# Heads of two pairs change places in the rows of y and x; past terms as products on quarters of the array

## The chip, the cores and the metric

The kernel runs on one core of a Trainium2 chip. The metric is the device time of one execution in microseconds; the median of three runs before the change is 200.99 us (200.46 to 201.04). Lower is better.

Words used below: TensorE multiplies matrices and writes to PSUM, an accumulator memory of banks of 2 KB per partition; VectorE (DVE), ScalarE (ACT) and GpSimd (POOL) do the elementwise work; SyncE (SP) issues most of the transfers (DMA), POOL those of k. A product has a stationary operand, loaded into the array beforehand (a weight load, PEld), and a moving one that streams through it. Where an operand has 64 rows (contraction) or 64 columns (output partitions), only half or a quarter of the 128 x 128 array is used, and products on different parts can run side by side; the profile writes such forms as rows*columns, 128*64, 64*128 or 64*64.

## The reference

```python
# q, k, v: (B=4, H=8, S=768, D=64)
gamma = 1.0 - 2.0 ** (-5.0 - np.arange(H))
for t in range(S):
    state = gamma * state + outer(k[t], v[t])         # per batch and head, 64 x 64
    y[t] = (1 / sqrt(D)) * (q[t] @ state)
x = y.transpose(0, 2, 1, 3).reshape(B * S, H * D)      # 3072 tokens x 512
h = x @ w_in                                           # 512 -> 2048
g = h * np.tanh(softplus(h))                           # mish
out = g @ w_out                                        # 2048 -> 512
```

## The kernel before

**Chunks and heads.** The 768 tokens of a batch are cut into 6 chunks (NCH) of 128 tokens (C), 24 chunks in all, numbered g. Within a chunk, y has a *present* term, from the masked scores of the chunk's own tokens, and a *past* term, q times the state that the chunk before handed on; a chunk that opens a batch has no past term. The 8 heads go in 4 pairs (HP); pair i holds heads 2i and 2i+1, of 64 columns each, so that a pair fills 128 partitions: row block 64*hh is head 2i+hh. The scaling by gamma is put into q and v when they are cast to fp16 (qs, vs).

**y and x.** y is built transposed in PSUM: partition is the row within a pair, then pair, chunk and token. Copied to fp16 it is xt, whose pair index is also the block of 128 rows of w_in (bp) that it meets in the first matrix product. So the order of heads within a pair is the order of the rows of w_in within a block.

**Blocks.** The first block takes 4 chunks, with its own layout of tokens (functions with `first` or `two` in their name), the ten others 2 chunks each, beginning at chunks 4, 6, 8 and so on to 22. For a block, g1_seven computes the product with w_in and seven the one with w_out, by seven products of halves in place of eight for most of the work, with sums of operands on VectorE (x_sums, win_sums, sums_a and so on). A table of steps (steps_of, steps_of_first) names places in those two functions ("p2", "p7", "m1", "m2", "m5", "m7") at which work of the next chunks is issued. Engines execute in the order in which this code issues.

**State.** Two layouts exist. A *wide* state is [128, pair, 128] with the two heads of a pair on the diagonal blocks and zeros elsewhere, so that one product on the whole array serves a pair. A *compact* state, stcs[g], is [128, pair, 64]: head 2i+hh at partitions 64*hh on. Through chunk 4 the states are wide (state_first, and outer_wide and decay_wide with the mask gcm). From chunk 5 on outer makes compact sums in PSUM, state_sum and state_decay (VectorE, POOL) make stcs[g], in three rotating buffers, and spread_state copies it by two ScalarE copies (L435) into one of three wide buffers stx that POOL has zeroed at the start (L112).

**y of a block.** y_two issues the present products of two chunks (present, L463: whole contraction of 128 tokens, 64 output partitions, so two halves of the columns side by side), then the outer products of two later chunks (outer_two, L412), then the past products (past, L454: 4 per chunk on the whole array). It is called at step "m7" inside seven, between two groups of products with w_out (L727); ScalarE copies y to xt (L500).

**Weights and loads.** load_w reads w_in in four slices of 512 columns into staging buffers of [128, 4 blocks, 512]; slices 0 and 1 in two transfers of 256 columns, slices 2 and 3 in one (L158). In SP's queue they stand behind q, k and v of the first block and ahead of w_out (L165), the q and v of chunks 4 and 5 (L140), the last quarter of w_out in two halves (L170, cast by ScalarE at L186) and the further loads. The first slice's first half is cast to fp16 by POOL (L176), the rest by VectorE.

Of the kernel before, what the change touches and what calls it, by code (L numbers as in the profile page):

```python
# [16 lines left out]
def kernel(  # L17
# [67 lines left out]
    stx = [cpool.tile([P, HP, P], FP16, name=f"stx{i}") for i in range(3)]  # L85
# [20 lines left out]
    nc.vector.memset(gcm, 0.0)  # L106
    for h in range(H):
        o = 64 * (h % 2)
        nc.vector.memset(gcm[o:o + 64, h // 2, o:o + 64], float(gamma[h] ** C))
        nc.vector.memset(gcv[o:o + 64, h // 2:h // 2 + 1], float(gamma[h] ** C))  # L110
    decay = gcv.unsqueeze(2).broadcast_to((P, HP, D))
    for t in stx:  # L112
        nc.gpsimd.memset(t, 0.0)
# [39 lines left out]
    def load_w(which, s):  # L153
        if which == "in":
            t = wstage.tile([P, NBP, TB], FP32, name="wi", tag="wt", bufs=4)
            n = TB // 2 if s < 2 else TB
            for o in range(0, TB, n):
                nc.sync.dma_start(t[:, :, o:o + n], win_ap[:, :, s * TB + o:s * TB + o + n])  # L158
        else:
            if s < NSL // 2:  # L160
                t = wstage.tile([P, FPS, d_model], FP32, name="wt", tag="wt", bufs=4)
            else:
                t = gp.tile([P, FPS, d_model], FP32, name="wt", tag="g")
            if s < NSL - 1:
                nc.sync.dma_start(t, wout_ap[:, s * FPS:(s + 1) * FPS])  # L165
        wtmps[which, s] = t
# [70 lines left out]
    def cast_two(nm, s, half):  # L237
        src = raw.pop((nm, s, half))
        if nm == "k":
            if s not in k16s:  # L240
                k16s[s] = castp.tile([P, 2, R, HP, D], FP16, name="qk16")
            nc.scalar.copy(k16s[s][:, half].rearrange("p r h d -> p h r d"), src)
        else:
            v16s[s, half] = castp.tile([P, R, HP, D], FP16, name="v16")
            nc.gpsimd.tensor_tensor(
                v16s[s, half].rearrange("p r h d -> p h r d"), src,
                vs_two[:, half * HP:(half + 1) * HP].unsqueeze(3).broadcast_to((P, HP, R, D)),
                op=ALU.mult)
# [56 lines left out]
    def present_first(s, y, pairs):  # L305
        for i in pairs:
            half, j = divmod(i, HP // 2)
            for r in range(R):
                for c in range(2):
                    for hh in range(2):  # L310
                        nc.tensor.matmul(
                            y[64 * hh:64 * hh + 64, c, i], v16s[s, half][toks(c), r, 2 * j + hh],
# [118 lines left out]
    def spread_state(g):  # L431
        states[g] = stx[g % 3]
        for hh in range(2):
            o = slice(64 * hh, 64 * hh + 64)
            nc.scalar.copy(states[g][o, :, o], stcs[g][o])  # L435

    def outer_wide(g):
        _, k16, v16, _ = cast[g]
        u_ps = u_tile()[:, 0]
        for i in range(HP):  # L440
            nc.tensor.matmul(
                u_ps[:, i], k16[:, 2 * i:2 * i + 2], v16[:, 2 * i:2 * i + 2],
                start=True, stop=True)
# [7 lines left out]
    def past(g, y):  # L451
        st, qt = states[g - 1], qkts[g][0]
        for i in range(HP):
            nc.tensor.matmul(  # L454
                y(i), st[:, i], qt[:, i], start=False, stop=True, skip_group_check=True)

    def present(g, y, fresh):
        am = ams[g]
        v16 = cast[g][2]
        for i in range(HP):  # L460
            for hh in range(2):
                o = 64 * hh
                nc.tensor.matmul(  # L463
                    y(i)[o:o + 64], v16[:, 2 * i + hh], am[:, hh, i],
# [242 lines left out]
    def seven(blk, steps, last):  # L707
# [53 lines left out]
        step("m5")  # L761
# [259 lines left out]
    def spread_next(g):  # L1021
        if g in stcs:
            spread_state(g)

# [6 lines left out]
    def steps_of(blk):  # L1031
# [3 lines left out]
        else:  # L1035
# [6 lines left out]
            "p7": [(store_due, 2), (sum_next, a - 2), (spread_next, a - 3), (sums_a, blk, slice(0, FPS))],  # L1042
# [5 lines left out]
            "m5": only((spread_next, a - 2)),  # L1048
# [4 lines left out]
    def steps_of_first(blk):  # L1053
# [8 lines left out]
            "m1": [(spread_next, a - 2), (scores, a - 2), (scores, a - 1), (mask, a - 2)],  # L1062
# [44 lines left out]
```

## Time and profile before

| what | value |
|---|---|
| median of three runs | 200.99 us |
| the profiled execution | 200.17 us |
| its span, first to last instruction | 198.4 us |
| granted TensorE clock | 1.00 |
| PE busy | 190.2 us, 96% of the span |
| DVE, ACT, POOL busy | 144.8, 114.9, 82.5 us |
| moved by DMA | 36.05 MB |
| past products on wide copies (L454 from stx) | 60, 4.9 us busy |
| past products of chunks 4 and 5 (L454 from st) | 8 |
| present products (L463) | 160, 6.4 us busy |
| copies of states (L435) | 30, 402 ns each, 57.7 to 178.7 us |

How to read it. The span is what the profile covers; the time of an execution has some 1.8 us more around it. Busy times of products overlap, since a product's record covers its passage through the array and the next one starts long before that ends; the step from one start to the next is what a product costs in a stream. In the timeline a line gathers a run of like instructions: start, time from the first start to the last end, engine, line, operation, the array form rows*columns, operand shape and count, and in brackets the idle time ahead of it with its releaser. In the chain of waits each piece has its start and its length; "SPq" is SP's queue of instructions, and DMA is a transfer that was waited for. In the table by windows the DMA share is the mean share of time for which the sixteen DMA engines had packets in hand; packets that overlap on an engine count twice, so it can exceed 1.

### The profile page before, as it was taken

To read this page: it belongs to the slowest core of one execution; us is meant where nothing else is said; L and a number is where in the kernel's file an instruction comes from. 1 tells how busy PE (TensorE), PEld (TensorE's weight loads), DVE (VectorE), ACT (ScalarE), POOL (GpSimd) and SP (SyncE) were. 2 spreads that over 40 slices of the span, in tenths; PEclk is the share of its full clock that TensorE was granted. 3 is DMA by queue.
4 is the path that set the end of the run, shared out by engine and by line. 5 is a ranking of instruction groups with operands and counts; after the bars stand their busy time and mean duration, and the time that the engine had idled before them with its cause. 6 is when DMAs were issued, how large, how long until landed. Compare 5 with 4: busy or idle time off the path is not lost.

```text
span 198.4 us, 5725 instructions
## 1 busy us (share of the span) xinstructions
PE 190.2 (96%) x2363; PEld 157.7 (79%) x2363; DVE 144.8 (73%) x294; ACT 114.9 (58%) x220; POOL 82.5 (42%) x110
## 2 busy tenths in 40 slices
PE   6897999999999999999999999999999999999992
PEld 2355546974987988988988988988988988988982
DVE  3786698998898597597498597597498596596362
ACT  2463667243673675675664774774754765765840
POOL 7072005695646708708606707707615614110000
PEclk9999999999999999999999999999999999999999
DMA  5999999999999999997997996997996967201102
GB/s 170 302 311 354 384 388 318 196 298 176 166 259 225 180 188 226 202 145 156 188 162 156 157 168 146 179 176 93 244 195 84 202 90 61 102 3 53 56 26 79
DMA packets 95897, 36.05 MB, mean 182 GB/s; under 512 B 82304, under 2 KB 89984, under 8 KB 95872
## 3 DMA queue, kind: packets, MB, share of 16 engines
q1 hardware_dynamic: 74928, 33.04, 76.3%
q0 software_dynamic: 20800, 2.62, 21.0%
q8 instruction: 18, 0.29, 0.7%
q14 instruction: 7, 0.06, 0.1%
q10 hardware_dynamic: 144, 0.03, 0.1%
HBM read 27.30 MB, written 6.29 MB: 169 GB/s over the span
## 4 chain that ended last, share of the span: by engine, by line
PE 78%; SPq 7%; DMA 6%; DVE 4%; ACT 2%; issue 1%; DVEq 0%
PE o_ps L727 30%; PE h_ps L654 18%; PE h_ps L630 16%; SPq L140 5%; DMA wt<-in_moe_w_out_dram 4%; PE y_ps L463 3%; PE at L397 3%; DMA qfirst<-in_q_dram 2%; PE y_ps L454 2%; PE o_ps L924 2%; PE h_ps L798 1%; SPq L165 1%; PE u_ps L412 1%; DVE gsum L705 1%; SPq L170 1%
## 5 line engine op out<-in xcount | busy, mean ns | idle before, releaser
L654 PE MATMUL h_ps<-xt,win 128*128 128x256 f16 x320 | 41.5, 273 | 0.0
L647 DVE TENSOR_TENSOR hsum<-h_ps,hsnap 128x512 f32<-128x512 f32 x30 | 19.8, 688 | 20.9 <-PE h_ps L630 18.9
L727 PEld LDWEIGHTS <-gsum 128*128 128x128 f16 x320 | 30.8, 98 | 4.0 <-DVE gsum L705 0.4
L654 PEld LDWEIGHTS <-win 128*128 128x128 f16 x320 | 29.3, 98 | 3.6
L727 PE MATMUL o_ps<-tmat,gsum 128*128 128x256 f16 x240 | 27.8, 273 | 0.0
L727 PEld LDWEIGHTS <-g 128*128 128x128 f16 x240 | 23.3, 98 | 2.9
L641 ACT ACTIVATE g<-hsum 128x512 f16<-128x512 f32 x30 | 18.6, 630 | 11.4 <-DVE hsum L647 11.2
L403 DVE TENSOR_TENSOR am<-at,tri 128x1024 f16<-128x1024 f32 x20 | 24.3, 1215 | 0.0
L347 POOL TENSOR_TENSOR v<-vf,qvs 128x512 f16<-128x512 f32 x20 | 23.5, 1177 | 0.4 <-PE o_ps L924 0.4
L661 ACT ACTIVATE g<-h_ps 128x512 f16<-128x512 f32 x40 | 22.9, 603 | 0.8 <-PE h_ps L654 0.6
L637 ACT COPY hsnap<-h_ps 128x512 f32<-128x512 f32 x30 | 16.4, 582 | 11.2 <-PE h_ps L630 11.2
L336 POOL TENSOR_TENSOR qk<-qf,qvs 128x512 f16<-128x512 f32 x20 | 21.6, 1080 | 2.1 <-DMA qf<-in_q_dram 2.1
L355 POOL COPY gate<-gsum 128x1 f16<-128x1 f16 x9 | 1.6, 183 | 48.4 <-DVE gsum L701 48.4
L741 DVE TENSOR_TENSOR osb<-o_ps,snap 128x256 f32<-128x256 f32 x30 | 12.5, 418 | 12.4 <-PE o_ps L727 10.9
L733 ACT COPY snap<-o_ps 128x256 f32<-128x256 f32 x30 | 11.2, 372 | 16.0 <-PE o_ps L727 15.7
L630 PEld LDWEIGHTS <-wsum 128*128 128x128 f16 x320 | 19.5, 98 | 0.5
L727 PE MATMUL o_ps<-wout,g 128*128 128x256 f16 x160 | 19.3, 273 | 0.0
L342 POOL DMA_DIRECT2D qk<-in_k_dram x20 | 18.8, 942 | 0.0
L630 PE MATMUL h_ps<-xsum,wsum 128*128 128x128 f16 x240 | 16.7, 219 | 0.0
L500 ACT CAST xt<-y_ps 128x1024 f16<-128x1024 f32 x10 | 10.1, 1013 | 10.6 <-PE y_ps L454 10.6
L630 PEld LDWEIGHTS <-win 128*128 128x128 f16 x240 | 15.1, 98 | 0.7
L435 ACT COPY stx<-stc 64x256 f16<-64x256 f16 x30 | 12.0, 400 | 2.0 <-POOL stc L429 1.8
(119 smaller groups left out, 306.9 us busy)
## 6 DMA issues: line engine op xcount, KB each, us to landing
vf<-in_v_dram SPq DMA_DIRECT2D x24, 256.0 KB, 5.7
out_dram<-osb SPq DMA_DIRECT2D x22, 256.0 KB, 4.9
qf<-in_q_dram SPq DMA_DIRECT2D x20, 256.0 KB, 5.4
wt<-in_moe_w_out_dram SPq DMA_DIRECT2D x3, 1024.0 KB, 8.9
qk<-in_k_dram POOLq DMA_DIRECT2D x20, 128.0 KB, 5.5
wi<-in_moe_w_in_dram SPq DMA_DIRECT2D x4, 512.0 KB, 7.3
wi<-in_moe_w_in_dram SPq DMA_DIRECT2D x2, 1024.0 KB, 11.3
qfirst<-in_q_dram SPq DMA_DIRECT2D x2, 512.0 KB, 5.1
```

The lines of the kernel that those rows point to most:

```text
L336: nc.gpsimd.tensor_tensor(room16(g)[0], loaded[g][0], qs.unsqueeze(2).broadcast_to((P, H, D)), op=ALU.mult)
L342: nc.gpsimd.dma_start(room16(g)[1], k[b, :, c * C:(c + 1) * C].rearrange("h p d -> p h d"))
L347: nc.gpsimd.tensor_tensor(room16(g)[2], loaded[g][2], vs.unsqueeze(2).broadcast_to((P, H, D)), op=ALU.mult)
L403: nc.vector.tensor_tensor(am, ats.pop(g), tri.unsqueeze(1).unsqueeze(1).broadcast_to((P, 2, HP, C)), op=ALU.mult)
L630: nc.tensor.matmul(h_ps[:, f], w(f, d), x(d), start=first and f == 0 and d == 0, stop=d == n - 1, skip_group_check=True)
L637: nc.scalar.copy(x, h_ps)
L641: nc.scalar.activation(gt[:, 2 * i * FPS:(2 * i + 1) * FPS, j * P:(j + 1) * P], h, AF.Mish, scale=inv_boost3)
L647: nc.vector.tensor_tensor(h, h_ps, x, op=ALU.add)
L654: nc.tensor.matmul(h_ps[:, j], win(s, 2 * half + j, bp), xt(blk, bp), start=bp == 0, stop=bp == NBP - 1)
L661: nc.scalar.activation(gt[:, fb:fb + 2], h_ps, AF.Mish, scale=inv_boost3)
L727: nc.tensor.matmul(o_ps, x(f), w(f), start=first and f == 0, stop=f == n - 1, skip_group_check=True)
L741: nc.vector.tensor_tensor(dst, o_ps, plus, op=ALU.add)
```

## The change

For pairs 2 and 3 the two heads change places in the rows of y, x and so of w_in: head 2i goes to the upper 64 partitions and head 2i+1 to the lower (`side`). Rows of the state, q and k stay where they are, so in pairs 2 and 3 a state's rows and its columns lie in different halves.

- past: from chunk 7 on, a product per head from the compact state (64 rows of contraction, 64 output partitions) in place of one per pair from a wide copy; pairs in the order 0, 2, 1, 3, so that four products running use the four quarters of the array. The buffers stx, their memsets, spread_state and its three places in the tables of steps go.
- present and present_first write each head's output to its new side; the mask gcm has its blocks there, and outer_wide makes its sums head by head, there.
- cast_two puts the heads of v's second half in swapped order, by two POOL instructions.
- load_w: blocks 0 and 1 of w_in in one transfer as before, blocks 2 and 3 in two transfers of 64 partitions that swap the halves; eighteen transfers in place of six.

```diff
-    stx = [cpool.tile([P, HP, P], FP16, name=f"stx{i}") for i in range(3)]
...
+    def side(i, hh):
+        o = 64 * (hh if i < HP // 2 else 1 - hh)
+        return slice(o, o + 64)
...
-        nc.vector.memset(gcm[o:o + 64, h // 2, o:o + 64], float(gamma[h] ** C))
+        e = side(h // 2, h % 2)
+        nc.vector.memset(gcm[o:o + 64, h // 2, e], float(gamma[h] ** C))
...
-    for t in stx:
-        nc.gpsimd.memset(t, 0.0)
...
-            n = TB // 2 if s < 2 else TB
+            n, hb = (TB // 2 if s < 2 else TB), NBP // 2
             for o in range(0, TB, n):
-                nc.sync.dma_start(t[:, :, o:o + n], win_ap[:, :, s * TB + o:s * TB + o + n])
+                src = win_ap[:, :, s * TB + o:s * TB + o + n]
+                nc.sync.dma_start(t[:, :hb, o:o + n], src[:, :hb])
+                for x in range(2):
+                    nc.sync.dma_start(
+                        t[64 * x:64 * x + 64, hb:, o:o + n],
+                        src[64 * (1 - x):64 * (1 - x) + 64, hb:])
...
+            if half == 0:
+                nc.gpsimd.tensor_tensor(dst, src, f, op=ALU.mult)
+            else:
+                for hh in range(2):
+                    nc.gpsimd.tensor_tensor(
+                        dst[:, 1 - hh::2], src[:, hh::2], f[:, hh::2], op=ALU.mult)
...
                     for hh in range(2):
+                        e = side(i, hh)
                         nc.tensor.matmul(
-                            y[64 * hh:64 * hh + 64, c, i], v16s[s, half][toks(c), r, 2 * j + hh],
+                            y[e, c, i], v16s[s, half][toks(c), r, 2 * j + e.start // 64],
...
-    def spread_state(g):
-        states[g] = stx[g % 3]
-        for hh in range(2):
-            o = slice(64 * hh, 64 * hh + 64)
-            nc.scalar.copy(states[g][o, :, o], stcs[g][o])
...
         for i in range(HP):
-            nc.tensor.matmul(
-                u_ps[:, i], k16[:, 2 * i:2 * i + 2], v16[:, 2 * i:2 * i + 2],
-                start=True, stop=True)
+            for hh in range(2):
+                nc.tensor.matmul(
+                    u_ps[:, i, side(i, hh)], k16[:, 2 * i:2 * i + 2], v16[:, 2 * i + hh],
+                    start=i == 0 and hh == 0, stop=True, skip_group_check=True)
...
     def past(g, y):
-        st, qt = states[g - 1], qkts[g][0]
-        for i in range(HP):
-            nc.tensor.matmul(
-                y(i), st[:, i], qt[:, i], start=False, stop=True, skip_group_check=True)
+        qt = qkts[g][0]
+        for i in (0, 2, 1, 3):
+            if g <= CPB + 1:
+                nc.tensor.matmul(
+                    y(i), states[g - 1][:, i], qt[:, i], start=False, stop=True,
+                    skip_group_check=True)
+                continue
+            for hh in range(2):
+                o = slice(64 * hh, 64 * hh + 64)
+                nc.tensor.matmul(
+                    y(i)[side(i, hh)], stcs[g - 1][o, i], qt[o, i], start=False, stop=True,
+                    skip_group_check=True)
...
-                o = 64 * hh
                 nc.tensor.matmul(
-                    y(i)[o:o + 64], v16[:, 2 * i + hh], am[:, hh, i],
+                    y(i)[side(i, hh)], v16[:, 2 * i + hh], am[:, hh, i],
...
-            "p7": [(store_due, 2), (sum_next, a - 2), (spread_next, a - 3), (sums_a, blk, slice(0, FPS))],
+            "p7": [(store_due, 2), (sum_next, a - 2), (sums_a, blk, slice(0, FPS))],
...
-            "m5": only((spread_next, a - 2)),
...
-            "m1": [(spread_next, a - 2), (scores, a - 2), (scores, a - 1), (mask, a - 2)],
+            "m1": [(scores, a - 2), (scores, a - 1), (mask, a - 2)],
```

## The prediction

> **What bounds the kernel now.** First the chain that ended last, on the page:
>
> ```profile
> PE 78%; SPq 7%; DMA 6%; DVE 4%; ACT 2%; issue 1%; DVEq 0%
> ```
>
> Four fifths of the span is TensorE, the rest mostly queue and transfers. The same chain in order of time shows where each rules:
>
> ```profile
> 22.83 0.37 SPq L165
> ...
> 25.58 5.21 SPq L140
> ...
> 36.80 7.38 DMA wt<-in_moe_w_out_dram
> ...
> 44.20 1.05 ACT wout L186
> ...
> 45.29 1.46 PE o_ps L924 x6
> ```
>
> The reader should see a border at 45.3 us. Before it, the chain runs through SP's queue, the landing of the last quarter of w_out (L170), its cast on ScalarE (L186), and only then TensorE (L924). TensorE is close behind: its sequencer idles 0.37 us ahead of L924 at 45.29 (the weight loads of the timeline), so a delay of the transfers passes on whole, while a gain of TensorE before 45.3 us buys nothing. After it every piece is TensorE's, up to the last sum and store; apart from 0.25 us at 62.99 it never waits, so there only TensorE's own work counts.
>
> The stretches, up to 45 us (columns: window; its length; busy time and count of PE, PEld, DVE, ACT, POOL; granted clock; DMA share; GB/s):
>
> ```profile
> 14.00:16.00 2.00, 1.75 (x48) 1.28 (x42) 2.00 (x3) 1.50 (x2) 1.70 (x3) 1.00 1.09 347
> 22.00:24.00 2.00, 2.00 (x11) 0.93 (x10) 1.19 (x3) 1.47 (x3) 0.00 (x0) 1.00 1.05 384
> 36.00:38.00 2.00, 2.00 (x21) 1.79 (x19) 2.00 (x4) 0.00 (x0) 1.18 (x2) 1.00 1.75 194
> ```
>
> The DMA share is above 1 in each two-microsecond stretch from 4 us on: the engines have no gap into which longer transfers could slip. The first two stretches carry w_in:
>
> ```profile
> wi<-in_moe_w_in_dram SPq DMA_DIRECT2D x4, 512.0 KB, 7.3
> wi<-in_moe_w_in_dram SPq DMA_DIRECT2D x2, 1024.0 KB, 11.3
> ```
>
> Last TensorE's timeline, in the first block and in a later one:
>
> ```profile
> 15.08 0.42 PE L274 MATMUL at<-qfirst_t,qkt 64*64 64x128 f16 x16 [0.25 <-DVE am L281]
> 15.43 0.62 PE L293 MATMUL u_ps<-v,qk 64*128 64x128 f16 x16
> ...
> 17.24 0.42 PE L311 MATMUL y_ps<-am,v 64*64 64x128 f16 x16
> 17.59 0.62 PE L318 MATMUL y_ps<-qfirst_t,st 128*128 128x128 f16 x8
> 18.05 0.27 PE L798 MATMUL h_ps<-xt,win 128*128 128x256 f16 x1
> ```
>
> ```profile
> 76.49 0.64 PE L463 MATMUL y_ps<-am,v 128*64 128x128 f16 x16
> 76.96 0.42 PE L412 MATMUL u_ps<-v,qk 128*64 128x64 f16 x16
> 77.31 0.62 PE L454 MATMUL y_ps<-qkt,stx 128*128 128x128 f16 x8
> 77.76 0.82 PE L727 MATMUL o_ps<-wout,gsum 128*128 128x256 f16 x6
> ```
>
> What to read is the step from one start to the next group's start. Sixteen products on quarters (64*64) took 0.35 us until another form followed, twice. Eight past products on the whole array took 0.45 to 0.46 us, with the next group of the same form.
>
> **The past terms (L451 to L455).** Where the state is compact (chunks from 7 on) four whole products of a chunk become eight on quarters. Blocks with two such chunks: those starting at chunks 8, 10, 14, 16, 20, 22, six in all. There 0.45 us becomes 0.35 us, the change of form back to whole products being within the 0.35. The change of form on entry is paid already: the step of L412 (0.35 us) holds it. So 6 x 0.10 = 0.60 us. Three blocks (6, 12, 18) have one such chunk, as the other opens a batch. There four whole products took 0.28 us (106.71 to 106.99). Eight quarters are 0.35 us less two rows of four quarters. Sixteen scores on halves (L397) took 0.55 us (70.59 to 71.14) for eight rows and one change of form; with L463's eight rows in 0.47 us, a row is about 0.06 us and a change 0.1 us. So 0.35 - 0.12 = 0.23 us, 0.05 less each, of which I take 0.02 as the row is rounded: 0.06 us together. Total about -0.65 us. Bounds: the quarters now pair the two products of one head pair in one PSUM bank, on other partitions, which L274 and L311 don't do. If only two quarters could run at a time, sixteen would take 8 x 0.06 + 0.10 = 0.58 us: 0.13 us dearer in six blocks and, with eight taking 0.34 us, 0.06 in three: +0.96 us. I take the L311 row, as it too accumulates into y.
>
> **The present term (L463) and the outer products.** Same count; in pairs 2 and 3 the two column halves come in the other order, so a half is used twice running three times a block. The products go two by two (0.47 us for sixteen is 8 x 0.06), and each two still use both halves: 0. If a half met its own predecessor each time and lost a row: 10 blocks x 3 x 0.06 = 1.8 us at most; half a row is as far as I'd go. outer_wide (L441) issues eight products of 64 columns in place of four of 128, once, at 43.93, ahead of the 0.37 us wait: nothing, and some 0.2 us (the step of eight such products, L412 in the chain at 48.73: 0.24 us) without that cover.
>
> **What goes away elsewhere.** 30 copies on ScalarE (L435, 402 ns, 12.0 us), some of them queued ahead of the snaps (L733). In the table of waits nothing on TensorE waits for either after 45 us, and L435's own answer names nobody who waited for it: 0. Three memsets on POOL (1.45 us) end at 4.5 us, and POOL then idles 5.17 us for v: 0. The compact state must now live until the past product has read it: its three buffers' next writer, L429 for the third chunk on, comes after the y of its block, so nothing new is waited for. VectorE's list is unchanged. On POOL v's second half is cast in two instructions twice; four of one measure 1.06 us, so two halves are 1.06 us and some overhead, and POOL had 0.30 us of idle time ahead of the next cast (L176 at 15.61). Were that used up, w_in's first cast and TensorE's L798 at 16.70 would slip by it, into the 0.37 us.
>
> **w_in's transfers (L153 to L158).** Six become eighteen: for each, one of 128 partitions with half of the bytes, and two of 64 partitions with a quarter each. Twelve more issues on SP: L158 took 0.83 us apiece, blocked by the full queue rather than by work, and L165 issues in 0.37 us, so 18 x 0.37 = 6.7 us against the 6.00 us that the six took; the transfers last longer than that, so it hides behind them. Behind them on SP are w_out (L165), q and v (L140) and the last w_out (L170): every one goes later if w_in does, and the chain above hangs on the last.
>
> No row shows a transfer with a destination of 64 partitions; all of this kernel's loads are 128 wide. Lower bound: rows are as long as before (1 KB and 2 KB), so the time is the same, 0; a gain is excluded, with engines above a share of 1. Upper bound: what reaches half of the partitions goes at half the rate. w_in is 4.19 MB; from 14 to 24 us the windows give 347, 346, 368, 387 and 384, mean 366 GB/s, so 11.5 us; half of its bytes at half of the rate add 5.7 us. Between them I go by the row with two streams on the same engines: at 36 to 38 us SP's loads and POOL's loads of k share them at 194 GB/s and a share of 1.75, so what shares a part of the path does not fit into spare room here. That puts me above the middle, at six tenths: +3.4 us. I hold this to be more likely than the 0, by which all sixteen engines would deliver as much to half of the partitions.
>
> The Trainium skill, SBUF — State Buffer, section "Door 1: The DMA port swizzle (why `[64,N]` ≈ `[32,N]`)", says that partitions 0 to 63 are reached by 8 of 16 ports and levels off near 218 GB/s for such a range. By that page alone, 2.1 MB would take 9.6 us in place of 5.7 us, an estimate of +3.9 us; no run here shows it yet.
>
> **Sum.** +3.4 - 0.65 = +2.75 us on the span, 198.4 to 201.2 us. The profiled execution took 200.17 us, 1.8 us around its span; the median of the runs is 200.99 us, 0.8 above it. On the median: 203.8 us.
>
> **Rivals.**
> 1. *Half-wide transfers cost nothing.* For it: same bytes, same row lengths, sixteen engines. Against it: no slack in the engines. Then only TensorE's gain is left: 200.99 - 0.65 = 200.3 us. This is the other side: it decides as soon as w_in's two 64-wide parts land together as fast as one of 128. About 0.3% of the time (0.6 us) is what a measurement of this kernel can tell from no change, so it sits on that border.
> 2. *Partly hidden:* engines that run ahead in the first 64-wide transfer are on the second while others still write the first. At a quarter of the upper bound: +1.4 - 0.65, 201.8 us.
> 3. *Quarters in one bank go two at a time,* transfers costing nothing: 200.99 + 0.96 = 202.0 us. Against it: L311's row. It would show at once as a stretch over 0.45 us for sixteen.
> 4. *The wait grows:* the full 5.7 us: 206.0 us. For it: the chain has no slack; against it: VectorE's and POOL's other work up to 45 us is not all behind w_in.
>
> **Chances.** Forecast 0.50, rival 1 0.32, rival 2 0.08, rival 3 0.04, rival 4 0.06. Rival 1 splits into 0.18 faster and 0.14 within the 0.3%; rival 2 leaves 0.02 within it and 0.06 slower; the rest is slower: faster 0.18, same 0.16, slower 0.66. I move 0.03 from slower to faster for work that leaves ScalarE. The range runs from rival 1 less 0.2 us, 200.1, to 205.2, some six tenths of the way from the forecast to rival 4; the forecast's own range is 202.8 (1 us less for the transfers) to 205.2.
>
> **What would show it.** For the transfers: 14 to 28 us at clearly under 347 to 387 GB/s; the landing of the last w_out after 47 us in place of 44.2; L924's second stage starting near 48.7. If these stay, rival 1 holds. For the past terms: 0.35 us between their start and L727's in two-chunk blocks; 0.58 is rival 3. L463's step staying at 0.47 shows the order of halves free. If SP idles between w_in's eighteen issues with the engines below a share of 1, the issues bind and my working was wrong.

## The result and the profile after

The changed kernel takes 207.35 us (median of six runs, 206.04 to 209.51) against 200.77 us for the kernel before (six runs beside it, 200.46 to 201.04): a ratio of 1.032, with an interval of 1.028 to 1.036. It is 6.6 us slower by these medians; 203.8 was forecast, and 205.2 was the end of the range. One of the six executions, 209.51, was a slow one; the ratio leaves it out, and the other five have a median of 207.02 us. The profiled execution took 207.02 us, with a span of 205.2 us. In its code every line quoted here lies 8 to 15 further down: L463 is now L478, L727 is L742, L630 is L645, L924 is L938, L186 is L194.

The chain that ended last, by engine:

```profile
PE 73%; DMA 14%; SPq 5%; DVE 2%; POOL 2%; issue 0%; POOLq 0%
```

TensorE's share fell from 78 to 73%, that of transfers rose from 6 to 14%. In order of time (start, length, what) the chain up to 45 us is now made of transfers, where SP's queue stood before:

```profile
12.55 6.17 DMA wi<-in_moe_w_in_dram
18.74 8.01 DMA wi<-in_moe_w_in_dram
26.77 15.17 DMA wt<-in_moe_w_out_dram
41.97 1.43 DVE wout L192
```

The windows of the same stretch (columns: window, length, busy time and count of PE, PEld, DVE, ACT and POOL, granted clock, DMA share, GB/s):

```profile
14.00:16.00 2.00, 1.75 (x49) 1.27 (x41) 2.00 (x3) 1.50 (x2) 1.49 (x3) 1.00 1.16 249
18.00:20.00 2.00, 1.47 (x30) 1.11 (x29) 0.31 (x1) 0.59 (x1) 0.00 (x0) 1.00 1.13 237
24.00:26.00 2.00, 2.00 (x11) 0.88 (x9) 0.56 (x1) 1.24 (x3) 0.00 (x0) 1.00 1.08 197
30.00:32.00 2.00, 2.00 (x7) 0.78 (x6) 1.84 (x5) 0.60 (x1) 0.00 (x0) 0.55 1.06 240
34.00:36.00 2.00, 2.00 (x11) 0.86 (x9) 1.87 (x4) 1.21 (x3) 0.00 (x0) 1.00 1.05 388
```

Read the last two columns together. The sixteen DMA engines have packets in hand all the time, as before (share above 1), and move 197 to 288 GB/s in every two-microsecond stretch from 14 to 34 us, where the kernel before moved 347 at 14 us and 384 at 22. At 34 us, with w_in in place, the rate is back at 388.

From issue to landing (columns: engine, count, size, median us):

```profile
wt<-in_moe_w_out_dram SPq DMA_DIRECT2D x3, 1024.0 KB, 14.5
wi<-in_moe_w_in_dram SPq DMA_DIRECT2D x8, 256.0 KB, 7.5
wi<-in_moe_w_in_dram SPq DMA_DIRECT2D x8, 128.0 KB, 5.9
```

The x8 of 256 KB mix the whole blocks of slices 0 and 1 with the halves of slices 2 and 3, which have the same size. Then ScalarE's casts of the last w_out (L186 before, at 44.20 us):

```profile
50.04 1.05 ACT L194 CAST wout<-wt 128x1024 f16<-128x1024 f32 x1 [2.08 <-DMA wt<-in_moe_w_out_dram]
51.49 1.05 ACT L194 CAST wout<-wt 128x1024 f16<-128x1024 f32 x1 [0.41 <-DMA wt<-in_moe_w_out_dram]
```

The last cast is 7.3 us later. TensorE still waits for it, as its weight loads show (L924 before, at 45.29 us):

```profile
52.59 0.96 PEld L938 LDWEIGHTS <-g 128*128 128x128 f16 x5 [0.23 <-issue]
```

The wait is now 0.23 us in place of 0.37, since a second path comes almost as late: the chain above goes on from the third quarter of w_out through VectorE (L192, L566) and POOL's casts of chunks 4 and 5 (L349, L360) to a turn on TensorE at 49.18 us. TensorE, in the first block and in a later one:

```profile
29.77 8.77 PE L530 MATMUL h_ps<-xt,win 128*128 128x512 f16 x32 [2.92 <-DVE win L184]
41.05 1.05 PE L938 MATMUL o_ps<-tmat,gsum 128*128 128x256 f16 x8 [1.64 <-DVE gsum L948]
...
57.08 1.06 PE L645 MATMUL h_ps<-xt,win 128*128 128x128 f16 x16
...
84.09 0.64 PE L478 MATMUL y_ps<-am,v 128*64 128x128 f16 x16
84.56 0.42 PE L425 MATMUL u_ps<-v,qk 128*64 128x64 f16 x16
84.91 0.42 PE L469 MATMUL y_ps<-qkt,stc 64*64 64x128 f16 x16
85.26 1.05 PE L742 MATMUL o_ps<-wout,gsum 128*128 128x256 f16 x8
```

In the first block it waits 2.92 us for w_in's casts. The granted clock is 0.55 to 0.59 from 30 to 34 us; as TensorE waits for VectorE again at 41.05, this is not on the path here. In the later block the steps are what the prediction wanted: 0.47 us for the present term, 0.35 for the outer products, 0.35 for sixteen past products on quarters (0.45 before for eight whole ones). From the first L645 (L630 before) to the end of the span it is 148.1 us instead of 148.6 (205.2 - 57.1 and 198.4 - 49.8). So the account of the two profiled executions closes: 7.3 us later at the border, 0.5 us less behind it, 6.8 us on the span. The profiled execution of the kernel before (200.17 us) was faster than any of its other executions on record, so differences against it are some 0.6 us larger than those of the medians.

### The profile page after: what moved, and what is told of

The parts are those of the page before. It is cut to its first block, busy times and chain, and to the rows that moved or that the text cites. A ratio compares the mean times of both kernels' runs of the same rounds, so it can differ in the third digit from the quotient of the medians.

```text
span 205.2 us, 5831 instructions
## 1 busy us (share of the span) xinstructions
PE 192.0 (94%) x2427; PEld 156.8 (76%) x2427; DVE 145.1 (71%) x294; ACT 104.4 (51%) x190; POOL 81.4 (40%) x109
## 4 chain that ended last, share of the span: by engine, by line
PE 73%; DMA 14%; SPq 5%; DVE 2%; POOL 2%; issue 0%; POOLq 0%
PE o_ps L742 30%; PE h_ps L669 17%; PE h_ps L645 15%; DMA wt<-in_moe_w_out_dram 7%; DMA wi<-in_moe_w_in_dram 7%; SPq L239 4%; PE o_ps L938 3%; PE at L410 3%; PE y_ps L478 2%; POOL qk L349 1%; PE y_ps L469 1%; PE u_ps L425 1%; POOL v L360 1%; DVE wout L192 1%; SPq L162 1%; DVE gsum L720 1%
## 5 line engine op out<-in xcount | busy, mean ns | idle before, releaser
L742 PEld LDWEIGHTS <-gsum 128*128 128x128 f16 x320 | 30.6, 98 | 5.0 <-DVE gsum L720 0.7
L742 PE MATMUL o_ps<-tmat,gsum 128*128 128x256 f16 x240 | 27.8, 273 | 0.0
L742 PEld LDWEIGHTS <-g 128*128 128x128 f16 x240 | 23.4, 98 | 2.8
L360 POOL TENSOR_TENSOR v<-vf,qvs 128x512 f16<-128x512 f32 x20 | 23.6, 1179 | 0.5 <-PE o_ps L938 0.3
L349 POOL TENSOR_TENSOR qk<-qf,qvs 128x512 f16<-128x512 f32 x20 | 21.6, 1080 | 2.2 <-DMA qf<-in_q_dram 2.2
L645 PEld LDWEIGHTS <-wsum 128*128 128x128 f16 x320 | 19.5, 98 | 0.5
L742 PE MATMUL o_ps<-wout,g 128*128 128x256 f16 x160 | 19.3, 273 | 0.0
L530 PE MATMUL h_ps<-xt,win 128*128 128x512 f16 x56 | 14.1, 416 | 2.9 <-DVE win L184 2.9
L645 PE MATMUL h_ps<-xsum,wsum 128*128 128x128 f16 x240 | 16.7, 219 | 0.0
L645 PEld LDWEIGHTS <-win 128*128 128x128 f16 x240 | 15.1, 98 | 0.7
## 6 DMA issues: line engine op xcount, KB each, us to landing
wt<-in_moe_w_out_dram SPq DMA_DIRECT2D x3, 1024.0 KB, 14.5
```

Of the source, the lines that this page charges most:

```text
L349: nc.gpsimd.tensor_tensor(room16(g)[0], loaded[g][0], qs.unsqueeze(2).broadcast_to((P, H, D)), op=ALU.mult)
L360: nc.gpsimd.tensor_tensor(room16(g)[2], loaded[g][2], vs.unsqueeze(2).broadcast_to((P, H, D)), op=ALU.mult)
L530: nc.tensor.matmul(h_ps[:, j], win(s, f, bp), xt(blk, bp), start=(bp == 0), stop=(bp == NBP - 1))
L645: nc.tensor.matmul(h_ps[:, f], w(f, d), x(d), start=first and f == 0 and d == 0, stop=d == n - 1, skip_group_check=True)
L742: nc.tensor.matmul(o_ps, x(f), w(f), start=first and f == 0, stop=f == n - 1, skip_group_check=True)
```

## The experiments

### Which part of the change costs the time

Three kernels. In the first, the kernel before loads w_in with two transfers of 64 partitions for blocks 2 and 3, without changing their places:

```diff
-                nc.sync.dma_start(t[:, :, o:o + n], win_ap[:, :, s * TB + o:s * TB + o + n])
+                src, hb = win_ap[:, :, s * TB + o:s * TB + o + n], NBP // 2
+                nc.sync.dma_start(t[:, :hb, o:o + n], src[:, :hb])
+                for x in range(2):
+                    nc.sync.dma_start(
+                        t[64 * x:64 * x + 64, hb:, o:o + n], src[64 * x:64 * x + 64, hb:])
```

> The kernel before with one edit: blocks 2 and 3 of each piece of w_in come in two transfers of 64 partitions, without changing places; everything else is as before, products included. Theory (what reaches only half of the partitions is slow, and the wait for w_out passes it on whole): the changed kernel is 6.6 us over before by the medians and has saved some 0.5 us on TensorE, so about 207.8 us here, windows from 14 to 33 us at 200 to 280 GB/s, last cast of w_out starting near 51.5 us. Rival (the loss comes from the products on quarters, the swapped casts or the order of the halves): 200.8 us, with the windows at 350 to 390 GB/s.

Measured: 207.12 us, ratio 1.0315 (1.030 to 1.033), 6.4 us over 200.72; the last cast of w_out starts at 51.25 us. Its windows show the same picture as the changed kernel's:

```profile
14.00:16.00 2.00, 1.75 (x54) 1.17 (x51) 2.00 (x3) 1.37 (x2) 0.90 (x2) 1.00 1.14 256
24.00:26.00 2.00, 2.00 (x11) 0.81 (x9) 0.17 (x1) 1.47 (x3) 0.00 (x0) 1.00 1.07 217
30.00:32.00 2.00, 2.00 (x6) 0.64 (x5) 1.54 (x5) 0.60 (x1) 0.00 (x0) 0.50 1.06 244
```

The transfers alone make the loss. In the second kernel there are as many of them, eighteen, but all 128 wide (against the edit above):

```diff
-                for x in range(2):
-                    nc.sync.dma_start(
-                        t[64 * x:64 * x + 64, hb:, o:o + n], src[64 * x:64 * x + 64, hb:])
+                for x in range(hb, NBP):
+                    nc.sync.dma_start(t[:, x:x + 1, o:o + n], src[:, x:x + 1])
```

> The kernel before with eighteen transfers of w_in, all of 128 partitions: blocks 0 and 1 together, block 2, block 3; the same sizes, rows and order of issues as in the changed kernel but for the width. Theory (width): 200.8 us, no different from before, w_in at 350 to 390 GB/s. Rival (the number of transfers, their issues on SP or their completions): near 207 us.

Measured: 200.99 us, ratio 1.002 (1.0005 to 1.0034), some 0.3 us over 200.72. So the number of issues is a cost of its own, but a small one (its DMA share falls to 0.94 at 18 us and to 0.87 at 22, so for a while SP's issues bind here); it is the width that counts. The third kernel is the changed one with w_in in its six transfers, so that the rows of blocks 2 and 3 do not fit the order of heads any more:

> The changed kernel with w_in loaded in six transfers of 128 partitions, so that blocks 2 and 3 keep the old order of rows and the products with them are not the reference's. Theory: only TensorE's gain is left, 0.10 us in each of six blocks and little in three: 200.2 to 200.4 us, and the last cast of w_out near 44.2 us. Rival (something else in the change costs time too, in the first block or through POOL's casts): 201 us and more.

Measured: 200.22 us, ratio 0.998 (0.9964 to 0.9994): 0.50 us less than 200.72. Everything in the change but the transfers gains half a microsecond.

### The swap in another place

If the heads have to change places, this can be done where y is copied to x (L500 before): the past products still use the four quarters, w_in stays as it was, and the copy turns the halves of pairs 2 and 3 back. With one of the copies on VectorE:

```diff
-        nc.scalar.copy(
-            xts[blk][:, :, :2 * C], y_ps.rearrange("p i j c -> p i (j c)"))
+        x, y = xts[blk][:, :, :2 * C], y_ps.rearrange("p i j c -> p i (j c)")
...
+        nc.scalar.copy(x[:, :n], y[:, :n])
+        nc.scalar.copy(x[:64, n:], y[64:, n:])
+        nc.vector.tensor_copy(x[64:, n:], y[:64, n:])
```

> A version that needs no change of w_in: y has the heads of pairs 2 and 3 swapped in PSUM from chunk 6 on, for the products on quarters, and the copy to x turns them back: pairs 0 and 1 by ScalarE as before, one half of pairs 2 and 3 by ScalarE and the other by VectorE. Everything of the first block is as before. Theory: TensorE's gain of about 0.5 us is kept and the copies (0.59 + 0.59 us on ScalarE and 0.69 us on VectorE in place of 1.01 us) hide in the 1.75 us until the next block's first product: 200.2 us. Rival (the copies come late for the first products or for VectorE's sums of x): 10 blocks x 0.2 us dearer, 202 us.

A miss, near the 202 us of its rival: 202.61 us, ratio 1.0096 (1.008 to 1.011). From its table of waits (engine, line, whom it waited for, us in all, times, longest):

```profile
DVE xt L510 <- ACT xt L509: 12.0, 9, 1.7
ACT g L650 <- DVE hsum L656: 13.0, 11, 1.4
ACT hsnap L646 <- PE h_ps L639: 10.4, 9, 1.6
```

VectorE's copy did not run beside ScalarE's but after it: 0.5 to 1.7 us of waiting in each block, and as VectorE works in order, its sums behind the copy came late, and then what ScalarE takes from them. At 82.89 us ScalarE's copy hsnap (0.58 us) stands in the chain, where before there was only TensorE. The expectation had taken the two copies as parallel. With all three on ScalarE (0.58 us each):

```diff
-        nc.vector.tensor_copy(x[64:, n:], y[:64, n:])
+        nc.scalar.copy(x[64:, n:], y[:64, n:])
```

> As the version that turns the heads back in the copy, but all three copies on ScalarE (0.59 us each, 1.77 in place of 1.01 us). Theory: the copy of pairs 0 and 1 comes first and is earlier than before, pairs 2 and 3 are needed 0.45 us later than pairs 0 and 1, so 200.2 to 200.5 us. Rival: the third copy is late for the second group of products of the next block by up to 0.3 us in each of nine blocks: 201 to 203 us.

Measured: 200.16 us (twelve runs, 199.49 to 200.56) against 200.54, ratio 0.9972 (0.9959 to 0.9986). VectorE's sum of x waits 0.2 us a block for the last copy (L510), and the table shows nothing on TensorE that waits for it:

```profile
DVE xsum L613 <- ACT xt L510: 1.7, 8, 0.2
```

This version computes what the reference does, keeps the gain of the change and drops its loss; it beats both kernels, by little.

### What a transfer to half of the partitions costs

A kernel that only loads w_in in several shapes and stores zeros; VectorE reads a column as each piece lands, so the distance of two reads is what a piece costs in a full queue.

> Loads alone, nothing of the computation: nine stages of loads of w_in in rows of 2 KB, each waiting for the stage before; zeros are stored as the output. Stages: all four blocks 128 wide (4.2 MB); blocks 0 and 1 128 wide with blocks 2 and 3 in lower and upper halves (4.2 MB, the changed kernel's way); blocks 2 and 3 alone 128 wide (2.1 MB); in lower and upper halves by turns; all lower halves, then all upper; lower halves on SP with upper on ScalarE's queue; only partitions 32 to 95 (1.0 MB); only 0 to 63 (1.0 MB); blocks 2 and 3 each in its own transfer 128 wide. Theory A (each partition is reached by a path of its own group, and a lower or an upper half reaches half of the paths): 370 to 390 GB/s for 128 wide, about 200 for halves by turns and for all lower then all upper, over 300 for partitions 32 to 95, and clearly over 200 with the two halves on two queues at once. Theory B (any transfer of 64 partitions is slow, whichever they are): 32 to 95 at about 200 like 0 to 63. Theory C (half is the whole of it): the second stage takes 5.5 us more than the first; if more, the mix costs beyond the halves.

VectorE's timeline (start, length, in brackets the wait ahead):

```profile
8.66 0.15 DVE L76 COPY seen<-w 128x1 f32<-128x1 f32 x1 [2.48 <-DMA w<-in_moe_w_in_dram]
11.37 0.15 DVE L76 COPY seen<-w 128x1 f32<-128x1 f32 x1 [2.56 <-DMA w<-in_moe_w_in_dram]
...
22.00 0.15 DVE L76 COPY seen<-w 128x1 f32<-128x1 f32 x1 [3.54 <-DMA w<-in_moe_w_in_dram]
25.76 0.15 DVE L76 COPY seen<-w 128x1 f32<-128x1 f32 x1 [3.61 <-DMA w<-in_moe_w_in_dram]
...
56.08 0.15 DVE L76 COPY seen<-w 128x1 f32<-128x1 f32 x1 [2.10 <-DMA w<-in_moe_w_in_dram]
58.40 0.15 DVE L76 COPY seen<-w 128x1 f32<-128x1 f32 x1 [2.17 <-DMA w<-in_moe_w_in_dram]
...
63.47 0.15 DVE L76 COPY seen<-w 128x1 f32<-128x1 f32 x1 [0.26 <-DMA w<-in_moe_w_in_dram]
64.15 0.15 DVE L76 COPY seen<-w 128x1 f32<-128x1 f32 x1 [0.53 <-DMA w<-in_moe_w_in_dram]
64.77 0.15 DVE L76 COPY seen<-w 128x1 f32<-128x1 f32 x1 [0.47 <-DMA w<-in_moe_w_in_dram]
```

The first pair of rows are slices of 1.05 MB, 128 wide: 2.71 us, 387 GB/s. The second are slices as the change loads them, half whole and half by halves: 3.76 us, 1.05 us more each, 4.2 us for the four of w_in. The third pair are blocks 2 and 3 (0.52 MB) with the lower half issued by SP and the upper by ScalarE's queue: 2.32 us, 226 GB/s; both by SP, one after the other, took 2.25 us. A second queue does not bring the two halves to run together. The last rows are partitions 32 to 95 alone, 0.26 MB in 0.62 to 0.68 us, some 400 GB/s; the stage before was still running beside them up to 63 us, and from 63.0 to 63.5 us the DMA engines moved 389 GB/s. Partitions 0 to 63 alone took 1.21 us, 217 GB/s, and upper halves one behind another 1.21 to 1.23 us (the fifth stage, 50.16 to 53.82 us). So it is not that a transfer is narrow, but that its 64 partitions are one of the two halves. The Trainium skill (SBUF — State Buffer, "Door 1: The DMA port swizzle (why `[64,N]` ≈ `[32,N]`)") has partitions 0 to 63 on 8 of 16 ports, with some 218 GB/s at most, and 64 to 127 on the other 8; the 217 agree, and so does the full rate across both.

By that, 32 to 95 should go at the full rate and the two ends at half of it, which would leave half of the loss. Tried in the kernel before:

```diff
+                for p0, p1 in ((32, 96), (0, 32), (96, 128)):
+                    nc.sync.dma_start(t[p0:p1, hb:, o:o + n], src[p0:p1, hb:])
```

> The kernel before with blocks 2 and 3 of w_in in three transfers each: partitions 32 to 95, 0 to 31, 96 to 127, rows in their old places. Theory (the lower and the upper 64 partitions have paths of their own; a transfer is slow where it uses one of them only): the middle one runs at full rate, the two of 32 partitions at half of it, so half of the bytes of the two-halves version are slow and half of its 6.4 us are lost: 203.9 us, 203 to 205. Rival (a narrow transfer is slow in proportion to its width): 32 partitions at a quarter of the rate, more lost than with halves: 208 us or more.

A miss: 206.59 us, ratio 1.031 (1.027 to 1.035), nearly as slow as the change, and with another limit beside the width. Its windows:

```profile
16.00:18.00 2.00, 1.40 (x37) 0.80 (x36) 1.27 (x2) 0.00 (x0) 1.04 (x1) 1.00 0.77 219
18.00:20.00 2.00, 1.18 (x28) 0.88 (x17) 0.61 (x1) 0.59 (x1) 0.00 (x0) 1.00 0.70 225
20.00:22.00 2.00, 1.86 (x13) 1.27 (x13) 1.26 (x3) 1.09 (x2) 0.00 (x0) 1.00 0.50 153
```

Here the share falls to 0.50: the DMA engines stand without packets. SP's timeline gives the reason:

```profile
17.81 0.43 SPq L159 DMA_DIRECT2D wi<-in_moe_w_in_dram  x1
18.29 2.46 SPq L161 DMA_DIRECT2D wi<-in_moe_w_in_dram  x3
20.79 0.43 SPq L159 DMA_DIRECT2D wi<-in_moe_w_in_dram  x1
```

The first two rows are the four issues of half a slice: 2.98 us on SP, for 0.52 MB that need 1.35 us at full rate. The issues bind. How much of the loss is theirs and how much that of the two ends was not told apart. In the changed kernel the three issues of such a group take 1.9 us where the queue has room, which would still let 276 GB/s pass, more than the 197 to 250 that most windows show, and its share does not fall below 1.02 from 4 to 34 us, so there they do not bind.

### Loads alone lose less than the kernel

The kernel loses 6.4 us (the split alone, by the medians) to 7.3 us (the last cast, between the two profiled executions), the four slices alone only 4.2. Was it what stands before and behind them in SP's queue? The queue of the first block (q, k, v, w_in, three w_out) three times, only loads: w_in in six transfers, as the change loads it, and in eighteen 128 wide; zeros are stored.

> Loads alone, nothing of the computation: SP's queue of the first block (q, eight of k and v, w_in, three of w_out) three times, each after all of the last has landed: w_in in six transfers 128 wide, in eighteen as the changed kernel has them, in eighteen 128 wide; zeros are stored as the output. In the kernel the stream was some 7 us late at w_out's first quarters; four slices of 2 KB rows by themselves lost 1.06 us each, 4.2 us. Theory D (the queue's own order does it: rows of 1 KB, the tails of w_in beside w_out): the second pass is 6.5 to 7.5 us longer than the first from its first k to its third quarter of w_out. Theory E (the loss beyond 4.2 us comes from what the engines read and write meanwhile): 4 to 5 us. The third pass is within 0.5 us of the first by both.

From the first k to the third w_out: 25.74, 30.73 and 26.18 us. Halves lose 5.0 us, the number 0.4. One and a half to two microseconds were still missing, and the engines' work was the next suspect. The same queue five times, with casts of 128 x 1024 on VectorE and ScalarE and products on TensorE beside it or not:

> Loads alone took 5.0 us longer with the halves, the kernel 7.0. This kernel stores zeros and has SP's queue of the first block five times: (1) w_in in six whole transfers, (2) with halves, (3) with halves while VectorE and ScalarE cast 128 x 1024 without pause, (4) the same with TensorE multiplying too, (5) whole, with all three at work; GpSimd reads a column as each slice lands. Theory F, the work of the engines on the same memory slows transfers once half of the partitions has to take the stream: from the landing of the last v to that of the third w_out, pass 3 or 4 takes at least 1.5 us more than pass 2, with windows of 195 to 250 GB/s as in the kernel, and pass 5 no more than 0.5 us over pass 1. Theory G, the engines' work does not matter, and the missing 2 us come from the kernel's order of waits and issues: passes 2, 3 and 4 agree within 0.5 us, near 270 GB/s in w_in.

GpSimd's reads of the last v and of the third w_out mark the ends of the passes; whole, halves with idle engines, halves with casts:

```profile
13.60 0.18 POOL L74 COPY seen<-kv 128x1 f32<-128x1 f32 x1 [13.16 <-DMA kv<-in_v_dram]
33.09 0.18 POOL L74 COPY seen<-wt 128x1 f32<-128x1 f32 x1 [2.54 <-DMA wt<-in_moe_w_out_dram]
43.35 0.18 POOL L74 COPY seen<-kv 128x1 f32<-128x1 f32 x1 [10.07 <-DMA kv<-in_v_dram]
67.15 0.18 POOL L74 COPY seen<-wt 128x1 f32<-128x1 f32 x1 [2.53 <-DMA wt<-in_moe_w_out_dram]
77.39 0.18 POOL L74 COPY seen<-kv 128x1 f32<-128x1 f32 x1 [10.05 <-DMA kv<-in_v_dram]
103.51 0.19 POOL L74 COPY seen<-wt 128x1 f32<-128x1 f32 x1 [2.55 <-DMA wt<-in_moe_w_out_dram]
```

19.49, 23.80 and 26.12 us; with TensorE too 26.47, and whole with all three at work 20.06. The casts seemed to cost 2.3 us, and the missing microseconds to be found. But the busy passes were also the later ones. The same with the passes in another order, and one engine at a time:

> With the engines idle, SP's queue of the first block with halves took 23.8 us from the landing of the last v to that of the third w_out; with VectorE and ScalarE casting it took 26.1. Five passes again, all with halves, zeros stored, in another order: (1) VectorE and ScalarE cast, (2) VectorE alone, (3) ScalarE alone, (4) TensorE alone, (5) idle. Theory F, the casts slow the transfers: (1) about 26.1 and (5) about 23.8 although the idle pass now comes last; of (2) and (3) at least one lies more than 1 us above (5). Theory H, what a later pass loses has to do with its place in the program and not with the engines: (5) is 25.5 or more, and the passes do not differ by more than 0.7 us. For TensorE alone I expect 24.0 to 24.5, since it added 0.35 us to the casts.

The first pass (both cast) and the last (idle):

```profile
13.62 0.18 POOL L74 COPY seen<-kv 128x1 f32<-128x1 f32 x1 [13.18 <-DMA kv<-in_v_dram]
38.17 0.18 POOL L74 COPY seen<-wt 128x1 f32<-128x1 f32 x1 [2.53 <-DMA wt<-in_moe_w_out_dram]
...
157.81 0.18 POOL L74 COPY seen<-kv 128x1 f32<-128x1 f32 x1 [10.66 <-DMA kv<-in_v_dram]
185.15 0.18 POOL L74 COPY seen<-wt 128x1 f32<-128x1 f32 x1 [2.37 <-DMA wt<-in_moe_w_out_dram]
```

24.55 us with casts and 27.34 idle: theory F is refuted, the slowest pass had no engine at work. That agrees with the Trainium skill (SBUF — State Buffer, "Who interferes with whom"), by which no transfer contends with a compute engine. Theory H has the place right, but the passes do differ (24.55, 24.54, 26.40, 26.44, 27.34).

What the slow passes share is seen in the landings. The trace records for each transfer sixteen parts that land by themselves. The table gives each pass's time from the last v (in the last two runs: from q) to the third w_out, its loss against a whole pass of the same run (e10, which has none and ran on another chip, against the 19.49 of e9; e7's whole pass took 19.52), and the largest distance between first and last part of a transfer. Each of these kernels was executed once:

```
kernel, pass                     us    loss  apart
e9   whole, idle               19.49     -    0.4
e9   whole, all three work     20.06    0.6   2.5
e9   halves, idle              23.80    4.3   0.7
e7   halves, idle              24.44    4.9   1.2
e10  halves, VectorE           24.54    5.1   0.8
e10  halves, both cast         24.55    5.1   0.8
e9   halves, both cast         26.12    6.6   2.8
e10  halves, ScalarE           26.40    6.9   2.9
e10  halves, TensorE           26.44    7.0   3.6
e9   halves, all three         26.47    6.4   4.2
e10  halves, idle              27.34    7.9   3.8
e11  halves, idle (2 passes)   30.49, 32.55   7.0, 9.1   4.5, 5.0
e12  halves, idle (2 passes)   31.11, 30.15   7.3, 6.4   4.7, 4.1
```

Whole transfers hardly mind if the parts are apart (0.6 us at 2.5). Halves cost 4.3 to 5.1 us where the parts stay within 1.2 us, and 6.4 us and more where they come apart by 2.8 and more, with no pass in between. In the changed kernel the distance is 0.9 us at 13 us and 4.1 us at 33, with the split alone it is 0.25 and 3.7, and the loss 6.4 to 7.3: it belongs to the second group. In the kernel before it is 0.8 us, and 1.7 from 19 us on, and costs nothing. Is being apart the cause? A small load into two partitions ahead of w_in was to make some parts late on purpose:

> The idle pass was the slowest of all, so the casts are not the cause. What the slow passes share is in the landings: every transfer lands in sixteen parts, and in the passes that took 23.8 to 24.6 us its first and its last part are 0.3 to 0.8 us apart, in those that took 26.1 to 27.3 us 1.4 to 4.2 us; in the changed kernel this grows from 0.9 us at 13 us to 4.1 us at 33. Theory I: as long as the parts run in step, lower and upper half of the partitions alternate and cost 4.3 to 5 us; once some parts are late, whole transfers meet halves of the one before, and both go slowly. Six passes here, engines idle, each behind a pause in which all transfers have landed; zeros stored: w_in (1) whole, (2) in halves, (3) whole behind a load of 64 KB into two partitions, which should make a few of the sixteen parts late by 1 to 2.5 us, (4) halves behind the same, (5) halves as in 2, (6) halves behind two such loads. From the landing of q to that of the third w_out, theory I: 2 and 5 lose 4 to 5 us on 1 and agree within 0.4; 3 loses up to 2.5 us on 1; 4 loses at least 1.5 us more on 3 than 2 loses on 1; and 6 more than 4. Theory J, the late parts are a consequence of the slowness and not its cause: 4 loses on 3 what 2 loses on 1, within 0.5 us. If the small load makes no part late, the run tells nothing of this.

> In the run before, the passes in halves that began in step did not stay so: single packets took 0.4 to 1.3 us between 36 and 45 us, first and last part of a transfer were 4 us apart without the small load, and the pass lost 7.0 us. So the two theories were not told apart. The same kernel with the passes in another order: (1) whole, (2) halves, (3) halves behind one small load, (4) halves, (5) halves behind one small load, (6) whole behind one. Theory I (parts out of step slow the halves): whatever pass stays within 1 us between first and last part loses 4 to 5 us on pass 1, and 3 and 5 lose at least 1.5 us more on 6 than that. Theory J (out of step is only a sign): 3 and 5 lose on 6 what 2 and 4 lose on 1, within 0.5 us, if 2 and 4 stay in step.

The load did make parts late, by 2.4 us. But in both runs the passes without it came apart by themselves (last rows of the table), so the condition of the test was not met. With it, halves lost 6.4 us in the first of the two runs (30.73 against 24.35 us for whole ones behind the same load), 7.0 and 7.1 us in the second (31.29 and 31.36 against 24.30). That is nearer to theory J than to the 1.5 us more of theory I, yet after the pause the queue also ran empty in these passes:

```profile
40.00:44.00 4.00, 0.00 (x0) 0.00 (x0) 1.00 0.80 207
```

(The twelfth kernel's second pass; columns: DVE, POOL, clock, share, GB/s.) The share of 0.80 puts a loss of another kind into these times, those of the last two rows of the table too. With two such loads the halves took 33.31 us, 2.6 more than with one; as the second load by itself landed 2.5 us after the first (168.76 and 166.25 us), this tells nothing either.

What comes just before the parts go out of step can be seen in the packets of the traces. Beside the data, the DMA engines carry packets of another kind; from the changed kernel's table of queues (packets, MB, share):

```profile
q8 instruction: 19, 0.31, 0.6%
```

In the changed kernel one of them, 16 KB, runs for 1.19 us from 15.78 us, the next for 1.24 us from 20.97; in the transfers that land after them the distance grows from 1.3 to 2.0 us, and then from 2.2 to 3.7. With the split alone it grows from 0.5 to 1.6 us after a packet at 15.62, and fifteen of the sixteen parts stay within 0.5 us: one part alone is late. The kernel before has such a packet at 16.68 us, and its distance goes from 0.8 to 1.7. In the two kernels with casts, too, the passes in step all lie ahead of the first such packet of their run (82.41 us in e9, 80.34 in e10), the others hold it or lie behind it. That is an order in time and not a test, and it is not the only origin: in the second passes of e11 and e12 no such packet is on record, and single packets of data took up to 1.3 and 1.5 us there. Why whole transfers bear a late part and halves do not, and whether it is the lateness that makes the halves slow, stays open.

## Why the prediction was wrong in size and right in mechanism

- **What bounds.** Right. The border at 45 us had no slack: the last cast of w_out comes 7.3 us later, and the span grows by this less TensorE's gain. One reading was wrong: behind the border not every piece is TensorE's. From 60.40 to 62.95 us the chain before runs through VectorE (L403, L705), and the 0.25 us at 62.99 are TensorE's wait for it; in the changed kernel this wait is 0.51 us (L742 for L720).
- **Past terms, -0.65 us.** Right for the six blocks with two chunks (0.35 us for sixteen quarters in place of 0.45). Eight quarters took 0.28 us from their start to L742's, as long as the four whole ones before (0.28), and not 0.23, so the 0.06 us of the other three blocks did not come. The sum was a little large: 0.50 us behind the border, and 0.50 us by the changed kernel with six loads. The quarters of one pair in one bank do run together, so rival 3 falls.
- **Present term, outer products, copies, memsets, v in two halves, at 0.** Right: the present term's step is still 0.47 us, behind the border nothing on TensorE waits for ScalarE, and with w_in in six transfers the longer waits behind it are the 0.51 us for VectorE named above and, in the profiled execution, its slowest (201.06 us), 0.49 us for a transposing transfer (qkt).
- **Twelve more issues at 0.** Nearly: 0.3 us in the kernel, 0.4 in the queue alone.
- **w_in's transfers, +3.4 us.** This term failed, and it alone. The mechanism was the one named: half of the partitions goes at half of the rate (217 against 387 GB/s). But its ends were no bounds. "Upper bound: what reaches half of the partitions goes at half the rate" put 5.7 us as the most, as if only the halves could be slowed. With the number of issues (0.3) taken off, the term measured 6.1 us by the medians (the split alone) and 7.0 at the last cast of the profiled executions. The upper bound's own rate was met: 4.19 MB in 11.5 + 5.7 us are 244 GB/s, and from 14 to 34 us the windows give 243 on the mean. But this rate held for 20 us and not for 17, over part of the w_out that stands behind (14.5 us from issue to landing) as well: by an estimate from these windows, 20 us at 243 in place of 366 GB/s are 20 x (1 - 243/366) = 6.7 us. In the loads alone the term was 4.3 to 5.1 us where the parts stayed in step, inside the bounds; why the kernel loses more stays open, as said above. The six tenths had no row behind them that shows such a transfer.
- **The 3.9 us by the Trainium skill** (SBUF — State Buffer, "Door 1: The DMA port swizzle (why `[64,N]` ≈ `[32,N]`)") is an estimate near the loads alone in step (4.2 for the four slices), and 2 to 3 us short of the kernel.
- **Sum.** 200.99 + 2.75 are 203.7 us and not 203.8, which changes nothing here.
- **Rivals.** Rival 4 (206.0 us, chance 0.06) came nearest, by its size: it too took the full 5.7 us as the most. Its counter-argument, that VectorE's and POOL's other work is not all behind w_in, did not hold, as w_out stands behind w_in in the same queue. Rival 1, the other side with 0.32, needed transfers that cost nothing; the kernel with six loads shows what it would have been, 200.2 us.
- **Signs.** All came as written for the transfers: under 347 GB/s, the last w_out after 47 us (51.5), L924's second stage later (52.6 instead of the 48.7 that the forecast had).

## What to carry to other kernels

A transfer whose partitions are 0 to 63 or 64 to 127 goes at little more than half of the rate here (217 against 387 GB/s), and a second queue does not help; where a layout needs the halves swapped, do it in a copy that is made anyway, and see that its parts do not wait for one another on two engines. When a chain runs through one full queue, a slower transfer can also be paid by what stands behind it: here the whole stretch of 20 us ran at the lower rate, so the bytes that are slow by themselves are no upper end of such a term. And an experiment with several passes has to give them in two orders before a difference is put down to what they do.

## What was not expected of the hardware

- Halves cost 4.3 to 5.1 us or 6.4 to 7.9 us for the same bytes and the same issues without a pause before w_in (e7, e9, e10), in two groups, with the sixteen parts within 1.2 us or 2.8 to 4.2 us apart; the cause is open.
- A packet of the kind `instruction`, 16 KB, ran for 1.14 to 1.17 us at 15 to 17 us in five kernels (e1, e2, e3, e4, e6); in the transfers that land after it one of the sixteen parts comes 1.2 to 1.5 us behind the other fifteen, which stay within 0.5 us.
- Two copies of the same PSUM tile to the same destination tile, on other partitions, did not overlap on ScalarE and VectorE (12.0 us of waiting in nine blocks). VectorE waited for a semaphore of ScalarE's; whether the chip needs this, or only the program's tracking of tiles asked for it, was not tried.
- SP needs 0.4 to 0.6 us for most issues, so three transfers of 64 to 128 KB behind one of 256 KB let the queue run empty (share 0.50).
- After 2.92 us without a product TensorE's granted clock was 0.55 to 0.59 for some four microseconds (30 to 34 us).
